# Half B of the first MoE layer and the whole second layer move from fp32r pairs to fp16 pairs, with gate tiles of 512 columns and layer 2 taken over quarters of d_ff

## The chip, the cores and the metric

One core of one Trainium2 chip (trn2). The metric is the device time of one execution in microseconds (us); lower is better. Five engines run side by side: TensorE (PE in the rows, with its weight loads as PEld), VectorE (DVE), ScalarE (ACT), GpSimd (POOL) and SyncE (SP), which here only issues DMAs.

## The reference, cut to what matters

```python
def _attn_ref(q, k, v, tau):                      # (4, 8, 576, 64), float32
    scores = 1.0 / np.sqrt(64) * np.matmul(q, k.transpose(0, 1, 3, 2))
    scores = np.where(scores >= scores.max(-1, keepdims=True) - tau, scores, -1e9)
    attn = softmax(scores)                        # with + 1e-09 under the division
    return np.matmul(attn, v)

def reference(...):
    x = attention, as (2304, 512)                 # tokens x d_model
    h = x @ moe_w_in                              # (512, 2048)
    x = (h * np.clip(h + 3, 0, 6) / 6) @ moe_w_out  # (2048, 512)
    h = x @ moe2_w_in
    return (h - np.tanh(h)) @ moe2_w_out
```

The four weight matrices come as float64; the kernel reads them as pairs of 32-bit words and makes float32 of them on ACT and DVE (`load_w`: one ACT and four DVE instructions of 512 columns for each 128 rows of d_ff).

## The kernel before, in words

Every product is made three times to keep float32 accuracy: each operand is a pair, a high and a low part, and high x high, high x low and low x high are added up in PSUM (`mm3`, L408). Before, both parts are fp32r tiles (float32 read in one pass).

The kernel has three stages, and a planner (`Plan`) writes out the order of every engine's instructions ahead of time: each task has an assumed duration, a key (a wanted start) and its buffers, and the planner plays them through and issues them in the order that comes out. On the chip the engines then run these queues strictly in order.

1. Attention, 144 units of 128 queries by 576 keys, with **half A** of layer 1 (the first 1024 of d_ff) woven in: PE makes scores (tile `s`), DVE takes the row maximum (L602), ACT the exponential (L604), DVE the cut (L613), POOL and ACT split the result into two fp16 parts, a DMA transposes them (`pt<-pp`), PE multiplies by v, itself an fp16 pair (`tp<-vt,pt`, L648). Half A's result goes to DRAM as `ys`, and its input as `xs`.
2. **Half B** of layer 1 (the other 1024 of d_ff): 9 blocks of 256 tokens x 8 tiles `m` of d_ff. `hidden` makes 12 matmuls of 256 columns into a PSUM tile (`m` or `h` by turns), `gate1` makes g on ACT and DVE (Relu L711, product L713, high part L718, low part L721), and `second` makes 12 matmuls of 256 columns into `ya`. Weights and x arrive as fp32r tiles; the blocks 0 and 1 take the first weights by turns, since the weights are still being made.
3. **Layer 2**, as Winograd's form of Strassen's product on blocks of 2 x 2: seven products of 6 matmuls of 256 columns, added up by DVE (`plus`, L1128) after an ACT copy (`keep`, L1123), then `gate2` (tanh L1135, difference L1136, L718, L721) and the output product with 3 matmuls of 512 columns for each tile of 128 tokens (`ya<-wo,g`). The stretches run over (half of d_ff, pair of token blocks p, quarter j of the half); the ninth block has a short stretch without Strassen. The parts of x are made in the first half, stored to DRAM (`xd..`) and read again in the second by POOL DMAs (L1111). The first half's partial output goes to DRAM (`po`, L1164) and is read and added in the second (L1169).

PSUM has two banks `m`, two `h` and four `ya`. The rings `R_t2` and `R_g2` hold the gates' tiles.

Of the kernel before, what the change touches and what calls it, by code (L numbers as in the profile page):

```python
# [43 lines left out]

class Ring:
# [16 lines left out]
class Plan:  # L62
# [13 lines left out]
    def add(self, eng, dur, key, fn, r=(), w=(), after=(), xfer=0.0, hold=False, slack=0.0, port=None):  # L76
        deps = dict.fromkeys(after)
# [111 lines left out]
def attention_moe_moe_kernel(  # L189
# [29 lines left out]
    nc = tc.nc  # L219
# [15 lines left out]
    HUGE = 122879.9921875  # L235

# [31 lines left out]
    three = const.tile([128, 1], F32, name="three")  # L268
# [12 lines left out]
    ident = at_p.tile([128, 128], F32, name="ident")  # L281
    ones = at_p.tile([128, 128], F32, name="ones")
# [56 lines left out]
    def load_w(kind, m, src, key, step, to, after=(), slack=0.0, scratch=None, cs=0.0, first=None, low="pool"):  # L339
# [12 lines left out]
        split_ = isinstance(to, list)  # L352

        def load():
# [5 lines left out]
            else:  # L360
# [4 lines left out]
            out=part(F32), in_=raw(1).bitcast(F32), func=ACTF.Abs), r=[wst], w=[wu], slack=cs if first is None else first)  # L365
# [10 lines left out]
                out=raw(1).bitcast(U32) if split_ else part(U32), in0=raw(0).bitcast(U32), scalar=29, in1=part(U32),  # L376
                op0=ALU.logical_shift_right, op1=ALU.bitwise_or),
        ]
        for n, f in enumerate(steps):
            add("dve", 0.65 if n > 1 or scratch else 0.5, key + 3 + n * step, f,  # L380
                r=[wu] if n < 2 else [wu, wst], w=[wst] if n == 3 and split_ else [wu], slack=cs, port=not scratch)
        if not split_:
            return add("dma", 0.47, key + 3 + 4 * step, lambda: nc.sync.dma_start(out=to, in_=part(F32)), r=[wu], xfer=0.8)
        n = DM // len(to)
        for h, W in enumerate(to):
            f32 = lambda h=h: raw(1)[:, h * n:(h + 1) * n].bitcast(F32)
            hi_lo(f32, W, [wst], key + 3 + 4 * step, step, n, cs, low)
# [10 lines left out]

    def flat(ap):
# [941 lines left out]
```

## Time and profile before

| | |
|---|---|
| time, three runs | 1111.94, 1113.19, 1115.34 us; median 1113.19 |
| the profiled execution | span 1113.7 us; no time of its own is listed beside the span |
| PE busy | 1047.2 us (94%), clock 0.975 of full on the mean |
| DVE, ACT, POOL busy | 825.4 (74%), 661.2 (59%), 352.3 (32%) us |
| DMA | 193.96 MB, mean 174 GB/s |
| chain that ended last | PE 80%, DVE 7%, DMA 5%, ACT 5% of the span |

PE's busy time is made of modelled ends of pipelined matmuls, so the mean duration of a matmul in the rows (395 ns for 512 columns) is longer than what one adds to the time; the start-to-start distance in a run of equal matmuls is what counts, and the chain of work that ended last gives it as a duration divided by a count.

### The profile page before, as it was taken

How to read it: one execution, taken by the hardware profiler on the slowest of the kernel's cores; microseconds unless marked ns; L12 is line 12 of the kernel's file. 1: busy time of each engine (PE TensorE's matmuls, PEld its weight loads, DVE VectorE, ACT ScalarE, POOL GpSimd, SP SyncE). 2: the span in 40 equal slices, each digit the busy share in tenths (PEclk: the TensorE clock that was granted, in tenths of full speed). 3: DMA queues.
4: the chain of work that ended last, by engine and by line, in shares of the span. 5: the costliest groups of instructions: out<-in, count | busy, mean ns of one | idle time of the engine just before them, and what ended most of it. 6: DMA issues, size and time to landing. Idle time of an engine off the chain costs nothing.

```text
span 1113.7 us, 23705 instructions
## 1 busy us (share of the span) xinstructions
PE 1047.2 (94%) x8912; PEld 975.8 (88%) x8912; DVE 825.4 (74%) x1761; ACT 661.2 (59%) x1420; POOL 352.3 (32%) x389
## 2 busy tenths in 40 slices
PE   5668799999999999989999999999999999999998
PEld 4557788998999899979999999988989898898887
DVE  5889977688878886757877776896796886656653
ACT  6867878688868886654544444654554564333332
POOL 2666757575766675662111100000000010010000
PEclk9858899999999999999999999999999999999999
DMA  7898678868987797778697765654732652543613
GB/s 182 164 224 203 132 180 168 188 130 189 171 173 134 176 146 152 168 214 250 208 292 242 231 195 169 236 180 141 266 130 86 227 202 77 187 136 83 193 47 95
DMA packets 283666, 193.96 MB, mean 174 GB/s; under 512 B 203424, under 2 KB 254112, under 8 KB 283552
## 3 DMA queue, kind: packets, MB, share of 16 engines
q1 hardware_dynamic: 268672, 166.50, 57.7%
q0 software_dynamic: 14256, 25.69, 8.1%
q8 instruction: 70, 1.15, 0.4%
q10 hardware_dynamic: 624, 0.26, 0.1%
q14 instruction: 44, 0.36, 0.1%
HBM read 96.99 MB, written 52.95 MB: 135 GB/s over the span
## 4 chain that ended last, share of the span: by engine, by line
PE 80%; DVE 7%; DMA 5%; ACT 5%; issue 2%; POOL 0%; SPq 0%; ACTq 0%; DVEq 0%; POOLq 0%
PE ya L408 26%; PE m L408 21%; PE h L408 10%; PE m L754 7%; PE s L597 7%; PE tp L648 6%; DVE e L613 2%; PE tp L480 2%; DMA pt<-pp 2%; DVE z L602 1%; DMA wdo<-wu 1%; DMA st<-in_moe_w_out_dram 1%; DMA st<-in_moe_w_in_dram 1%; ACT e L604 1%; ACT pp L618 1%
## 5 line engine op out<-in xcount | busy, mean ns | idle before, releaser
L408 PE MATMUL ya<-wo,g 128*128 128x512 f32 x864 | 238.0, 395 | 0.3 <-ACT g L718 0.3
L622 POOL TENSOR_TENSOR pp<-e,pp 128x128 f16<-128x128 f32 (+3 forms) x160 | 185.0, 1177 | 121.5 <-ACT pp L618 59.0
L408 PEld LDWEIGHTS m<-x,wi 128*128 128x128 f32 x1392 | 187.3, 189 | 12.5 <-ACT t L1123 0.3
L408 PE MATMUL m<-x,wi 128*128 128x256 f32 x1392 | 194.6, 281 | 0.1
L408 PEld LDWEIGHTS ya<-wo,g 128*128 128x128 f32 x864 | 146.7, 188 | 19.7 <-DVE wu L1169 0.8
L602 DVE TENSOR_REDUCE z<-s 128x1 f32<-128x576 f32 x144 | 108.4, 754 | 54.2 <-PE s L597 53.2
L408 PEld LDWEIGHTS h<-x,wi 128*128 128x128 f32 x1008 | 135.8, 190 | 7.8
L408 PE MATMUL h<-x,wi 128*128 128x256 f32 x1008 | 141.7, 282 | 0.0
L718 ACT ACTIVATE g<-t 128x256 fp32r<-128x256 f32 x216 | 89.4, 415 | 69.7 <-DVE t L1136 47.5
L613 DVE SCALAR_TENSOR_TENSOR e<-s,z,e 128x576 f32<-128x576 f32 x144 | 116.2, 812 | 15.4 <-ACT e L604 10.0
L408 PE MATMUL m<-xT,ai 128*128 128x256 f32 (+1 forms) x768 | 120.9, 303 | 3.1 <-DVE t L713 1.9
L597 PE MATMUL s<-ks,q 128*128 128x288 f32 x512 | 105.6, 335 | 18.7 <-DVE e L613 18.1
L721 DVE TENSOR_TENSOR g<-t,g 128x256 fp32r<-128x256 f32 x216 | 91.0, 422 | 40.5 <-ACT g L718 36.7
L408 PE MATMUL ya<-g,wo 128*128 128x256 f32 x864 | 115.6, 283 | 3.9 <-ACT g L718 3.2
L604 ACT ACTIVATE e<-s,z 128x576 f32<-128x576 f32 x144 | 105.5, 739 | 22.9 <-DVE z L602 18.3
L1135 ACT ACTIVATE t<-t 128x256 f32<-128x256 f32 x128 | 53.4, 417 | 106.5 <-DVE t L1128 105.9
L408 PEld LDWEIGHTS ya<-g,wo 128*128 128x128 f32 x864 | 108.3, 190 | 5.1 <-ACT g L718 3.8
L408 PEld LDWEIGHTS m<-xT,ai 128*128 128x128 f32 x768 | 107.5, 192 | 5.2 <-DVE t L713 2.7
L597 PEld LDWEIGHTS s<-ks,q 128*128 128x128 f32 x512 | 81.8, 211 | 25.8 <-issue 13.0
L648 PE MATMUL tp<-vt,pt 128*128 128x65 f16 (+1 forms) x2240 | 88.0, 199 | 9.3 <-DMA pt<-pp 6.2
L648 PEld LDWEIGHTS <-pt 128*128 128x128 f16 (+1 forms) x2240 | 79.6, 104 | 17.9 <-DMA pt<-pp 8.5
L618 ACT ACTIVATE pp<-e 128x1152 f16<-128x1152 f32 (+1 forms) x80 | 85.1, 1063 | 8.5 <-DVE e L613 7.0
(124 smaller groups left out, 1543.8 us busy)
## 6 DMA issues: line engine op xcount, KB each, us to landing
st<-in_moe_w_in_dram SPq DMA_DIRECT2D x32, 512.0 KB, 4.7
st<-in_moe_w_out_dram SPq DMA_DIRECT2D x32, 512.0 KB, 4.5
x<-xs POOLq DMA_DIRECT2D x36, 256.0 KB, 6.6
y<-y SPq DMA_DIRECT2D x18, 512.0 KB, 4.0
xs<-xT SPq DMA_DIRECT2D x8, 640.0 KB, 4.9
y<-ys SPq DMA_DIRECT2D x9, 512.0 KB, 5.8
po<-wu SPq DMA_DIRECT2D x18, 256.0 KB, 2.0
wu<-po SPq DMA_DIRECT2D x18, 256.0 KB, 2.9
```

Source lines behind the costliest of these rows:

```text
L408: nc.tensor.matmul(ps, l[a], r[b], start=first and t == 0 and i == 0, stop=last and t == 2 and i == n - 1,)
L597: nc.tensor.matmul(ps.t[:, half, 0:SH], l, ks[:, half * SH:(half + 1) * SH], start=i == 0, stop=i == len(ops) - 1,)
L602: add("dve", 0.69, key, lambda: nc.vector.tensor_reduce(out=z.t[:, 0:1], in_=s(), axis=AX.XY, op=ALU.max, negate=True), r=[ps], w=[z])
L604: exp = add("act", 0.66, key, lambda: nc.scalar.activation(out=ex(), in_=s(), func=ACTF.Exp, bias=z.t[:, 0:1]), r=[ps, z], w=[e])
L613: add("dve", 0.74, key, lambda: nc.vector.scalar_tensor_tensor(out=ex(), in0=s(), scalar=z.t[:, 1:2], in1=ex(), op0=ALU.is_ge, op1=ALU.mul ...
L618: high = add("act", t_act(w * S, sbuf=True), key, lambda: nc.scalar.activation(out=pp.t[:, 0:w, 0:S], in_=e.t[:, 0:w, :], func=ACTF.Copy), ...
L622: add("pool", t_pool(w * (src.stop - src.start)), key, lambda src=src, dst=dst: nc.gpsimd.tensor_tensor(out=pp.t[:, 0:w, dst], in0=e.t[:, ...
L648: nc.tensor.matmul(pv.t[0:m, w_ * (D + 1):(w_ + 1) * (D + 1)], pt.t[:, n, blk, rows], vv, start=o == 0, stop=o == len(ops) - 1)
L718: hi = add("act", t_act(n, sbuf=True), key, lambda: nc.scalar.activation(out=gh(), in_=t(), func=ACTF.Copy), r=[bt], w=[bh])
L721: add(low, t_pool(n) if low == "pool" else t_dve(n), key, lambda: eng.tensor_tensor(out=gl(), in0=t(), in1=gh().bitcast(F32), op=ALU.subtr ...
L754: prev = [add("pe", t_mm(n, 1), kd, lambda p=p, l=l, r=r, m=m, s=s, ps=ps: nc.tensor.matmul(ps.t[:, 0:n], W["o", m].t[:, l, s], r[m].t[:, ...
L1135: add("act", t_act(n), key, lambda: nc.scalar.activation(out=s_(), in_=h.t[:, 0:n], func=ACTF.Tanh), r=[h], w=[u])
```

## The change

Half B and layer 2 use fp16 tiles for both parts. An fp16 has a small range, so every operand is divided by a power of two found from the data (the row sums of its magnitudes, or for half B's weights the row maxima), and the gates undo it. The parts of the change:

- **The scales cross the partitions by PE.** ACT sums the magnitudes of a row (`row_sums`; for the weights of half B, 16 new loads `look` during attention with a DVE maximum each). `highest` turns the 128 sums into one row by a PE transpose, DVE takes the maximum, `everywhere` multiplies the one number by a row of ones on PE so that it stands on all partitions, and DVE makes the power of two. There are 24 such crossings: 9 for x in half B, 5 for x in layer 2, 10 for weights. They use the banks `m`.
- **fp16 matmuls**: 1728 of 256 columns in half B, 1536 of 256 and 864 of 512 in layer 2, as many as before. In the program each is now a weight load and a matmul; an fp32r matmul is one instruction that loads its own weights.
- **Gates of 512 columns**: one PSUM bank holds two tiles of d_ff, so half as many ACT and DVE instructions, each twice as wide; the ones with a scale per partition read it as an operand.
- **Layer 2 in four quarters** of d_ff, each with two tiles j at once; a stretch (quarter, p) has 84 matmuls of 256 columns and 48 of 512. The parts of x stay on chip for all four, so the stores and reads of `xd` go. Partial outputs are stored once (quarter 0), then added into DRAM by 36 accumulating DMAs from POOL (quarters 1 and 2), and read back in quarter 3. Their tiles `o` have three buffers.
- 18 of layer 2's 32 weight loads run in half B (28 before), the others in layer 2 up to the third quarter.
- x of half B is read by SP (before: POOL), then scaled and split (one ACT sum, one ACT copy and two DVE instructions of 1024 columns for each of 9 blocks).

The order on PE in the middle of layer 2, before: matmuls of `x` and `wi` into `m` and `h` (a Strassen product, 6 each) and output matmuls into `ya`.

```order
L408 MATMUL ya<-wo,g 128x512 x3
L408 MATMUL m<-x_14020,wi 128x256 x6
L408 MATMUL ya<-wo,g 128x512 x3
L408 MATMUL h<-x_14038,wi 128x256 x6
L408 MATMUL ya<-wo,g 128x512 x6
```

The same place now, at the seam between a Strassen product and the outputs; a product has 12 pairs and the outputs behind it 6.

```order
L472 LDWEIGHTS wi
L472 MATMUL m<-x_11486,wi 128x256
L472 LDWEIGHTS g
L472 MATMUL ya<-wo,g 128x512
...
L472 LDWEIGHTS wi
L472 MATMUL h<-x_11486,wi 128x256
```

Each matmul now has a weight load of its own in PE's queue; products and outputs alternate as before, in runs twice as long.

The order on PE around a crossing in half B, now (`xmax` holds the row sums of a block of x, `one` the maximum, `bw` and `bo` the weights); before, nothing stood between such runs of matmuls.

```order
L472 LDWEIGHTS bo
L472 MATMUL ya<-g,bo 128x256
L452 MATMUL m<-ident,xmax 1x128
L472 LDWEIGHTS bw
L472 MATMUL m<-xh,bw 128x256
...
L459 MATMUL m<-one,ones 128x1
L472 LDWEIGHTS bo
```

The transpose and the spread stand 12 pairs apart in this place; PE's queue stops at L452 if ACT's sum is late and at L459 if DVE's maximum is.

The order on POOL in layer 2: before, it read the parts of x again; now it adds the partial outputs `po` of 128 x 512 into DRAM.

```order
-L1111 DMA x_13485<-xd0T_184 128x1024
-L1111 DMA x_13505<-xd0X_185 128x1024
-L1111 DMA x_13525<-xd0T_186 128x1024
...
+L1413 DMA po_105<-o 128x512
+L1413 DMA po_106<-o 128x512
+L1413 DMA po_103<-o 128x512
```

31 reads went, 36 accumulating stores came; each frees a buffer `o` that an ACT copy waits for.

The diff, cut to its core:

```diff
+    def row_sums(src, dst, junk, r, w, key, n, cs=0.0):
+
+        return add("act", t_act(n, sbuf=True) + 0.19, key, lambda: nc.scalar.activation(
+            out=junk(), in_=src(), func=ACTF.Abs, scale=TOP, accum_out=dst), r=r, w=w, slack=cs)
...
+    def highest(src, top, key, after, ring):
+
+        bank = ring.new()
+        x = add("pe", 0.3, key, lambda: nc.tensor.transpose(bank.t[0:1, 0:128], src, ident), w=[bank], after=after)
+        return add("dve", 0.26, key + 0.1, lambda: nc.vector.tensor_reduce(
+            out=top, in_=bank.t[0:1, 0:128], axis=AX.X, op=ALU.max), r=[bank], w=[bank], after=[x])
+
+    def everywhere(top, key, after, ring, dur, fn):
+
+        bank = ring.new()
+        x = add("pe", 0.1, key + 0.2, lambda: nc.tensor.matmul(
+            bank.t[:, 0:1], ones[0:1, :], top, start=True, stop=True), w=[bank], after=after)
+        return add("dve", dur, key + 0.3, lambda: fn(bank.t[:, 0:1]), r=[bank], w=[bank], after=[x])
...
-    def mm3(ps, pairs, first=True, last=True, passes=(0, 1, 2)):
+    def mm3(ps, pairs, first=True, last=True, passes=(0, 1, 2), third=0, swap=0):
...
-            a, b = ((0, 0), (0, 1), (1, 0))[t]
+            a, b = ((0, 0), (swap, 1), (1, third))[t]
...
+        if far:
+            go = lambda: nc.vector.scalar_tensor_tensor(
+                out=gl(), in0=gh(), scalar=1.0 / GS2, in1=t(), op0=ALU.mult, op1=ALU.subtract)
+        else:
...
+            add("dma", 0.47, key, load, w=[wst], after=after, xfer=1.75, slack=ST)
+            seen[kind].append(add("dve", 0.69, key + 8.0, lambda: nc.vector.tensor_reduce(
+                out=mx[:, 5 + m:6 + m], in_=wst.t.rearrange("p (n t) -> p n t", t=2)[:, :, 1].bitcast(F32), axis=AX.X,
+                op=ALU.max, apply_absolute_value=True), r=[wst], slack=SB))
...
-        R_wi = ring2("slot1", 2 * MH, [128, 2, KD // 2, 128], F32R, "wi", 20)
-        R_wo = ring2("slot1", MH, [128, 2, DM], F32R, "wo", 2)
-        R_x2 = ring2("x2", 4, [128, 2, KD // 2, NB], F32R, "x2", 4)
-        R_t2 = ring2("g2", 2, [128, NB], F32, "t", 5)
-        R_g2 = ring2("g2", 3, [128, 2, NB], F32R, "g", 5)
-        R_f = ring2("big", 0, [128, 2, DM], F32, "f", 1)
-        R_c = ring2("big", 0, [128, DM], F32, "c", 4)
-        R_y = ring2("big", 0, [128, KD, NB], F32, "y", 3)
...
+        R_t2 = ring2([128, 2 * NB], F32, "t", tg=5, big=2)
+        R_g2 = ring2([128, 2, 2 * NB], F16, "g", tg=6, slot2=4)
+        R_bw = ring2([128, 2, DM], F16, "bw", slot1=MH)
+        R_bo = ring2([128, 3, DM], F16, "bo", slot1=MH)
...
+        R_wi = ring2([128, 2, 7, 2 * 128], F16, "wi", big=4)
+        R_wo = ring2([128, 3, DM], F16, "wo", big=8)
+        R_x = ring2([128, 2, 7, 2 * NB], F16, "x2", big=1, slot2=3)
...
+        R_o = ring2([128, DM], F32, "o", slot2=3)
...
+            a = row_sums(lambda: part(0), xmax[:, i:i + 1], lambda: x.t[:, 0, :, 0:n], [xf], [x], key - 10.0, KD * n)
+            a = common(xmax[:, i:i + 1], top_x[i % 2], xpow[:, 0, i:i + 1], xpow[:, 1, i:i + 1], 2.0 ** -6, key - 9.0, [a])
+            s = xpow[:, 1, i:i + 1]
+            hi = add("act", t_act(KD * n, sbuf=True, scalars=True), key - 6.0, lambda: nc.scalar.activation(
+                out=x.t[:, 0, :, 0:n], in_=part(0), func=ACTF.Copy, scale=s), r=[xf], w=[x], after=[a])
+            lo = add("dve", t_dve(KD * n, scalars=True), key - 5.0, lambda: nc.vector.scalar_tensor_tensor(
+                out=part(0), in0=part(0), scalar=s, in1=x.t[:, 0, :, 0:n],
+                op0=ALU.mult, op1=ALU.subtract), r=[x], w=[xf], after=[hi])
+            add("dve", t_dve(KD * n, scalars=True), key - 4.5, lambda: nc.vector.scalar_tensor_tensor(
+                out=x.t[:, 1, :, 0:n], in0=part(1), scalar=s, in1=part(0),
+                op0=ALU.mult, op1=ALU.add), r=[xf], w=[x], after=[lo])
+            u = lambda k: unscale[:, k, i:i + 1]
...
+            for a, m in enumerate(ms):
+                w = W["i", m]
+                pairs = lambda w=w: [
+                    ((w.t[:, 0, cols(kk)], w.t[:, 1, cols(kk)]), (x.t[:, 0, kk, 0:n], x.t[:, 1, kk, 0:n]))
+                    for kk in range(KD)]
+                turn[:] = [add("pe", t_half(n, 3 * KD), key + a * PM, lambda a=a, pairs=pairs: mm3(
+                    ps.t[:, a * n:(a + 1) * n], pairs(), first=a == 0, last=a == len(ms) - 1),
+                    r=[w, x], w=[ps], after=turn[-1:])]
+                hid.append(turn[-1])
+            gate1(lambda: ps.t, lambda: t.t, lambda: g.t[:, 0], lambda: g.t[:, 1],
...
-        order2 = [(half, p, j) for half in range(2)
-                  for p in ([0, NP2, *range(1, NP2)] if half == 0 else [*range(NP2), NP2]) for j in range(MQ)]
...
+        order2 = [(q, p) for q in range(NQ) for p in (first_order if q == 0 else [*range(NP2), NP2])]
...
-                xd[p, name] = dram.tile([128, 2, KD // 2, NB], F32, name=f"xd{p}{name}")
-                x_kept[p][name] = add("dma", 0.6, key + i + 2.0, lambda x=x, name=name: nc.sync.dma_start(
-                    out=xd[p, name], in_=x.t.bitcast(F32)), r=[x], xfer=1.6, slack=CF)
...
-        def again(p, key, after_y, after):
-
-            out = {}
-            for i, (name, stored) in enumerate(x_kept[p].items()):
-                x = out[name] = R_x2.new()
-                add("pool", 1.0, key + i - 6.0, lambda x=x, name=name: nc.gpsimd.dma_start(
-                    out=x.t, in_=xd[p, name].bitcast(F32R)), w=[x], after=[stored, *after], xfer=1.6, port=False)
-            return out
-
...
+            pair(lambda: ys_[0].t, four, [ys_[0]], [x], key - 2.0, 4 * n, s, ready, CL, CL, 0.2)
+            for i, name in enumerate(rows):
+                if name in ("X11", "X21"):
+                    continue
+                make(name, key + 2 * i - 3.0)
+                k = at_piece[name]
+                put = lambda h, k=k: x.t[:, h, k].rearrange("p (k n) -> p k n", k=2)
+                pair(src[name][0], put, [src[name][1]], [x], key + 2 * i - 2.0, 2 * n, s, ready, CL, CL, 0.2)
...
+            add("dve", t_dve(2 * NB, scalars=True), key, lambda: nc.vector.scalar_tensor_tensor(
+                out=s_(), in0=s_(), scalar=inv, in1=h.t, op0=ALU.mult, op1=ALU.subtract), r=[h, u], w=[u])
...
+            if q < NQ - 1:
+                add("act", t_act(DM, scalars=True), key, lambda: nc.scalar.activation(
+                    out=o.t, in_=a.t[:, 0:DM], func=ACTF.Copy, scale=sc), r=[a], w=[o], after=[ready])
+                if q == 0:
+                    po_stores[tile_] = add("dma", 0.47, key, lambda: nc.sync.dma_start(
+                        out=po[tile_], in_=o.t), r=[o], xfer=0.8)
+                else:
+                    po_stores[tile_] = add("pool", 1.0, key, lambda: nc.gpsimd.dma_start(
+                        out=po[tile_], in_=o.t, accum_op=ALU.add), r=[o], after=[po_stores[tile_]], xfer=1.6, port=False)
                 return
...
+            tiles = [(t, 0) for t in range(nb * nt)]
+            tiles += [(t, 1) for t in [*range(half, nb * nt), *range(half)]]
+            for t, a in tiles:
+                for j in range(MQ):
```

## Rows read from the trace of the kernel before

**Rows 1.** Busy time by stage: stretch, length, engines, clock, DMA share, GB/s.

```profile
core 0: us, PE busy (x) PEld busy (x) DVE busy (x) ACT busy (x) POOL busy (x), PEclk, DMA share, GB/s
290.00:450.00 160.00, 154.60 (x1763) 147.04 (x1762) 121.48 (x240) 119.64 (x224) 102.31 (x105) 1.00 0.81 155
512.00:600.00 88.00, 84.12 (x684) 82.92 (x683) 68.57 (x154) 41.44 (x91) 14.39 (x20) 0.98 0.86 262
600.00:690.00 90.00, 90.00 (x761) 90.00 (x760) 64.83 (x149) 40.01 (x92) 5.74 (x8) 1.00 0.64 202
722.00:930.00 208.00, 207.59 (x1317) 186.96 (x1317) 163.58 (x407) 113.05 (x283) 4.28 (x8) 1.00 0.49 174
930.00:1106.00 176.00, 175.99 (x1095) 157.41 (x1094) 103.65 (x249) 62.31 (x160) 12.17 (x23) 1.00 0.39 117
```

**Rows 2.** The chain that ended last: start us, us, what.

```profile
516.89 11.79 DMA st<-in_moe_w_out_dram
...
760.59 0.71 PE m L408 x6
...
763.43 2.79 PE ya L408 x12
...
1104.36 4.21 PE ya L408 x18
1108.57 0.02 issue
1108.59 0.69 DVE wu L1169
```

**Rows 3.** What PE waited for, 290 to 450, then 512 to 1114: us, times, longest.

```profile
PE s L597 <- DVE e L613: 1.6, 2, 0.8
PE tp L648 <- DMA pt<-pp: 1.6, 2, 1.3
...
PE ya L408 <- ACT g L718: 3.5, 3, 2.2
PE ya L408 <- DVE g L721: 0.4, 1, 0.4
```

**Rows 4.** Timeline of PE, 115 to 121: start us, us, what, count.

```profile
115.29 2.03 PE L648 MATMUL tp<-vt,pt 128*128 128x65 f16 x56
117.25 0.79 PE L597 MATMUL s<-ks,q 128*128 128x288 f32 x4
117.88 0.60 PE L480 MATMUL tp<-ident,qr 128*128 128x128 f32 x4
118.24 1.68 PE L408 MATMUL m<-xT,ai 128*128 128x256 f32 x12
...
120.28 0.28 PE L547 MATMUL tp<-vs,ones 128*128 128x1 f32 x2
120.42 0.84 PE L408 MATMUL m<-xT,ai 128*128 128x256 f32 x5
```

**Rows 5.** Groups by form: count | busy us, mean ns | idle before.

```profile
L547 PE MATMUL tp<-vs,ones 128*128 128x1 f32 x32 | 5.7, 248 | 2.6 <-ACT vt L545 1.5 <-DVE z L610 0.7 <-DVE m L367 0.4
L512 DVE SCALAR_TENSOR_TENSOR q<-tp,tau_b,q 128x512 fp32r<-128x512 f32 x32 | 23.8, 745 | 1.3 <-ACT q L510 1.3
L1095 DVE TENSOR_TENSOR c<-y 128x512 f32<-128x512 f32 x9 | 6.2, 685 | 0.0
L367 DVE TENSOR_SCALAR wu<-wu 128x512 f32<-128x512 f32 x48 | 24.0, 501 | 17.1 <-ACT wu L364 14.8
```

**Rows 6.** Timeline of DVE in layer 2: start us, us, what.

```profile
900.08 0.42 DVE L396 TENSOR_TENSOR wi<-c,wi 128x256 fp32r<-128x256 f32 x1
900.42 0.42 DVE L1136 TENSOR_TENSOR t<-t 128x256 f32<-128x256 f32 x1
900.75 0.42 DVE L396 TENSOR_TENSOR wi<-c,wi 128x256 fp32r<-128x256 f32 x1
```

**Rows 7.** What DVE waited for, 290 to 450.

```profile
DVE z L602 <- PE s L597: 22.7, 23, 3.9
```

**Rows 8.** DMA issues: count, KB each, median us from issue to landing.

```profile
st<-in_moe_w_in_dram SPq DMA_DIRECT2D x32, 512.0 KB, 4.7
x<-xs POOLq DMA_DIRECT2D x36, 256.0 KB, 6.6
po<-wu SPq DMA_DIRECT2D x18, 256.0 KB, 2.0
x<-xd0T POOLq DMA_DIRECT2D x4, 512.0 KB, 6.5
```

More of the change, by code (lines that the diff above doesn't have):

```diff
@@ L267, in attention_moe_moe_kernel @@
     tau_b = const.tile([128, 4], F32, name="tau_b")
-    three = const.tile([128, 1], F32, name="three")
+    NBL = len(blocks)
+    wm_t = const.tile([128, 2 * (5 + MH) + 8 * (5 + MH // 2)], F32, name="wmax")
+    widths = [(x, 5 + MH) for x in ("bi", "bo")] + [(k + str(q), 5 + MH // 2) for k in "io" for q in range(4)]
+    wmax = {x: wm_t[:, sum(w for _, w in widths[:i]):sum(w for _, w in widths[:i + 1])] for i, (x, _) in enumerate(widths)}
+    xmax = const.tile([128, NBL], F32, name="xmax")
+    xpow = const.tile([128, 2, NBL], F32, name="xpow")
+    unscale = const.tile([128, 2, NBL], F32, name="unscale")
+    ymax = const.tile([128, NBL], F32, name="ymax")
+    ypow = const.tile([128, 2, NBL], F32, name="ypow")
+    hid_s = const.tile([128, 2, 2, NBL], F32, name="hid_s")
+    out_s = const.tile([128, 2, NBL], F32, name="out_s")
+    one = const.tile([128, 4], F32, name="one")
+    three = const.tile([128, 2], F32, name="three")
+    ident = const.tile([128, 128], F32, name="ident")
+    ones = const.tile([128, 128], F32, name="ones")
     ps_m = ctx.enter_context(tc.tile_pool(name="ps_m", bufs=1, space=PSUM))
@@ L905, in load_x, with common @@
+        top_x = [one[0:1, a:a + 1] for a in range(2)]
+        def common(src, top, p, inv, c, key, after):
+            x = highest(src, top, key, after, R_m)
+            return everywhere(top, key, [x], R_m, 0.45, lambda b: power(b, p, inv, c))
+        def load_x(i, c, n, key):
+            xf, x = R_xf.new(), R_xh.new()
             after = writers(c, n)
+            part = lambda i: xf.t[:, i, :, 0:n]
             for h in range(2):
-                x = R_x2.new()
-                xs_.append(x)
@@ L947, in attention_moe_moe_kernel @@
+        for o, (kind, src) in enumerate((("i", w1_in), ("o", w1_out))):
+            for m in range(MH):
+                W = WB[kind, m] = (R_bw if kind == "i" else R_bo).new()
+                load_w(kind, MH + m, src, start - FW + WBO + WBS * (MH * o + m), 0.8, [W], late, cs=CB, first=CB1,
+                       put=scaled_pair(wmax["b" + kind][:, 2:3], scaled["b" + kind], kind == "o"))
         key = T2
         steps, xb, accs, before = [], {}, {}, {}
-        work = [(x, m) for m in range(MH // 2) for x in (0, 1)]
@@ L1217, in go @@
+                            third=2),
+                            r=[W, g], w=[ps], after=prevs.get((q, p, t), ()))
+                        prevs[q, p, t] = [x]
                         if l:
-                            finish(half, (2 * p * NB) // 128 + t, ps, key + 1.0)
+                            finish(q, (2 * p * NB) // 128 + t, ps, key + 1.0)
                     outs.append(go)
             return outs
+        nf = [NF]
+        for x in range(2):
+            record_prepare(x, [L2 - PK[2 * x], L2 - PK[2 * x + 1]], [[hid[-int(PK[2 * x] / 2.6) - 8]], [hid[-int(PK[2 * x + 1] / 2.6) - 8]]])
```

580 lines of the change are left out of this document (353 added, 227 removed).

## The prediction

> **What bounds the kernel now.** I read the busy time by stage first, because the change leaves attention nearly alone and rebuilds the rest. Attention ends near 512 us. From there PE is busy for all but 4 us of the first 88, and then for practically every microsecond to the end, at a granted clock of 1.00, the full of its two levels (2.4 GHz), while VectorE is busy 72 to 79% of the time and falls to 59% at the end, and the DMA engines 64%, then 39% [rows 1]. So behind 512 us a microsecond counts if it is PE's. The chain that ended last says the same: links of PE only, six matmuls of 256 columns in 0.71 us (118.3 ns each), twelve of 512 in 2.79 and eighteen in 4.21 us (233 ns each) [rows 2]; the stage from 600 us counts 761 in 90.00 us, 118.3 again [rows 1]. The sum is closed with these: 1728 + 1536 matmuls of 256 columns take 386.1 us and 864 of 512 take 201.3, together 587.4, and from 511.9 to the last matmul's end at 1108.6 us there are 596.7. Some 9 us are lost: PE waited 3.9 us for the gates [rows 3], mostly at 528 us, where a load of half B's weights took 11.79 us to land [rows 2], and the rest is spread.
>
> **fp16 matmuls.** The count of matmuls and columns stays, so what matters is what one adds. Between 256 and 512 columns an fp32r matmul costs (233 - 118.3) / 256 = 0.448 ns per column and 3.6 ns besides. The clock of 2.4 GHz would give 0.417 ns per column. The fixed 3.6 ns is small although each matmul loads new weights: that load lies beside the stream. I take it that the fp32r operand, not the array, makes the 0.031 ns per column more, and that fp16 streams at the clock with the same 3.6: 110.3 and 216.9 ns. That saves 3264 x 8.0 = 26.1 us and 864 x 16.1 = 13.9 us, **40.0 us**. No row shows an fp16 matmul of this width. The nearest is attention's, 65 columns wide: 56 from 115.29 to 117.25 us, 35.0 ns each [rows 4], and 65 columns at the clock are 27.1. If 7.9 ns is what a pair of weight load and matmul adds at any width, the new costs are 114.6 and 221.2 ns and the saving 22.3 us. Without any fixed cost (106.7 and 213.3) it is 54.9 us. If the column costs fp16 as much as fp32r, it is nothing. I take 40 because at 65 columns the stream is too short to hide a load, and at 256 it is four times as long; the ends are 0 and 54.9.
>
> Here the Trainium skill speaks on both sides. "TensorE: Matmul & The Clock Gate", section "Back-to-back issue gap", gives N/2.4 + 2.5 ns for a warm matmul; by that the saving would be an estimated 44.6 us. The same section says that a sustained stream of pairs of weight load and matmul takes about 81 ns at 128 columns, 25 more than that formula; 25 ns on each matmul here would be an estimated 131.7 and 238.3 ns, a loss of 48 us. The 35.0 ns of the fp16 pairs here, which leave 7.9 over the stream, speak against so much.
>
> **The crossings.** PE gets 24 transposes to one row and 24 spreads. In attention four transposes take (118.24 - 117.88) / 4 = 0.09 us each, and a spread by ones, which stands as two records, 0.14 us [rows 4]. That is 24 x 0.23 = **5.5 us**, on the path since PE has no gaps. Each also makes PE, which runs its queue in order, wait for ACT's sum and then for VectorE's maximum; behind it stand all products and outputs. Attention has the same construction 16 times, and PE idled 2.6 us ahead of it, 0.16 each [rows 5]. The planner puts 3 to 84 matmuls between the two halves in most places, none in four. From 0 to 2 x 24 x 0.16 = 7.7 us; I take one wait for each crossing, **3.9 us**.
>
> **The looks.** 16 loads of 512 KB and 16 maxima of 512 columns come into attention's last third. The maximum has no row; a VectorE instruction of 512 columns is 0.685 us [rows 5], together 11 us. VectorE waits 22.7 us for PE's scores between 290 and 450 us [rows 7], which covers them. The DMA engines are 81% busy there [rows 1], and a load of this size lands in 4.7 us [rows 8]; the transposes `pt` queue behind them. PE now waits only 1.6 us for those and 1.6 us for VectorE [rows 3]. From 0 to 11 us; I take **2 us**, near the bottom because both queues have room. If it is gone, scores come late first.
>
> **The start of half B.** Before, each tile m needed both its weights at once, and one late load stopped PE [rows 2]. Now all eight input weights come first, and the first output weight is needed only 84 pairs (9.3 us) after the start. I give back half of the 3.9 us waited, **2 us**; the ends are 3.9 back and 4 lost, if the eight output weights, which VectorE must now make in one run, are late.
>
> **The gates, x and weights on ACT and VectorE** I cost at nothing, with PE as cover. VectorE's work falls a little in sum (half as many gate instructions: 0.685 us for 512 columns, 0.745 with a scale per partition [rows 5], against 2 x 0.42 [rows 6]), but is uneven. Counting its rows in the new order at these durations, the full stretches of the first quarter, which also split x, take 18.6, 21.0 and 16.8 us, and two of the second quarter, in which the third is prepared, 20.8 and 23.8. PE needs 84 x 0.1103 + 48 x 0.2169 = 19.7 us for a stretch. Independent VectorE instructions start 0.33 us apart though each lasts 0.42 [rows 6]; 0.085 less for some 32 instructions leaves 16 to 21 us. It just fits; half B counts 189 us so, 160 without the overlap, against 190.6 of PE. The removal of the `xd` traffic (62 transfers of 512 KB) frees no PE time: the DMA engines were at 39 to 49% [rows 1].
>
> **The sum**, against the profiled execution: 1113.7 - 40.0 + 5.5 + 3.9 + 2 - 2 = 1083.1 us. Its span is 0.5 us over the median of the three runs, so **1083 us** stands for a run (1082.6, rounded). By its own terms the forecast runs from 1060 (54.9 saved, no crossing waits) to 1102 (all waits at their upper ends).
>
> **Rivals.**
> 1. *VectorE takes PE's place as the bound* in the first two quarters and at the end of half B. For it: the counts above, and a queue in order, where four chained instructions of a weight (the first 0.50 us, [rows 5]) stand ahead of a gate. If durations do not overlap, four stretches exceed PE's 19.7 us by 1.3, 1.1, 4.1 and 0.2, 7 us together, and with 5% of half B (9 us) PE loses 16: 1099 us. Against it: at 72 to 79% VectorE stopped nothing before. 15%.
> 2. *The weight load shows*: 22.3 us saved instead of 40, 1101 us. 8%.
> 3. *An fp16 column costs what an fp32r column does*: nothing saved, 1123 us, slower. The rows leave it open, since no wide fp16 matmul was run; the trace gives no other reason for 0.448 ns at full clock. 6%, with the 131.7 ns of the skill's sentence in it.
> 4. *The accumulating DMAs hold up the gates* (slower). In quarters 1 and 2 a stretch finishes four tiles `o`, with three buffers. Between the first and the fourth finish lie 18 output matmuls and two products, 3.9 + 2.6 = 6.5 us; the fourth ACT copy waits for the first tile's DMA, and behind it on ACT stand copies and gates. PE needs that bank 3.9 us later. So a DMA that lands within 10.4 us costs nothing, and each microsecond over it costs one in eight stretches; 30.6 us are eaten at 14.2 us. POOL's plain transfers of 256 KB landed in 6.6 us, SP's in 2.0, POOL's of 512 KB in 6.5 [rows 8]; an accumulating one has no row. At 16 us the time would be 1128. 6%. The Trainium skill, "SBUF — State Buffer", section "SBUF: two separate sides", says that GpSimd cannot write the descriptors of its DMAs while VectorE runs an instruction that takes both ports, a reason for such a delay; no row here separates it.
> 5. *The looks crowd attention's transposes* and take most of the gain: near 1110. 5%.
>
> **How the numbers follow.** The forecast has 60%. A change of under 0.3% (3.3 us) is about what runs of this kernel cannot tell from none. Faster: 60 + 15 + 8 and half of rival 5, 85%. Same: the rest of rival 5 and what lies between the cases, 5%. Slower: rivals 3 and 4 with their slighter forms, 10%. For the range I go down to 1062, just over the forecast's own floor, and up to 1104, which takes in rivals 1 and 2 at their prices; outside are rivals 3 to 5 and the upper half of rival 1's spread, 2 in 10.
>
> **What would show it.** In the new chain, twelve matmuls of 256 columns should be 1.32 us and three of 512 0.65; 1.42 and 0.70 would prove rival 3, 1.37 rival 2. PE's waits behind 512 us should name L452 and L459 with some 4 us, and the gates with a few; VectorE names in tens of microseconds would be rival 1, an ACT copy into `o` that waited for a DMA rival 4, with the landing time of `po<-o` beside it. Attention should end 0 to 4 us later than 512. I am wrong if PE idles over 15 us behind attention, or if the column of fp16 is not at the clock.

## The result, and the profile after

The changed kernel takes **1097.88 us** (median of four runs, 1096.08 to 1098.64) against 1112.57 us before (1111.20 to 1115.34), a ratio of 0.9857 with a 95% interval of 0.9832 to 0.9882. Its profiled execution took 1096.08 us, with a span of 1094.3 us.

The chain that ended last, in the kernel after (start us, us, what), answers to [rows 2]:

```profile
1071.10 5.18 PE ya L472 x24
1076.28 2.62 PE m L472 x24
1078.90 10.37 PE ya L472 x48
1089.27 0.03 issue
1089.30 0.75 DVE o L1418
```

Twenty-four matmuls of 256 columns take 2.62 us, 109.2 ns each, and 48 of 512 take 10.37 us, 216.0 ns each, where before it was 118.3 and 233. The end is still PE's.

Busy time by stage, kernel after (columns as in [rows 1]; the first five lines are its attention and the last half-A group, the others lie behind the start of half B):

```profile
330.00:360.00 30.00, 29.46 (x343) 28.12 (x340) 23.27 (x47) 23.45 (x47) 19.40 (x21) 1.00 0.86 189
360.00:390.00 30.00, 25.22 (x261) 22.34 (x260) 26.53 (x52) 22.53 (x41) 17.47 (x17) 0.83 0.91 196
390.00:450.00 60.00, 58.44 (x632) 56.09 (x631) 47.91 (x93) 42.53 (x79) 36.21 (x38) 1.00 0.96 198
450.00:480.00 30.00, 28.41 (x332) 27.09 (x332) 19.95 (x47) 16.98 (x34) 15.76 (x16) 1.00 0.92 211
480.00:512.00 32.00, 23.50 (x182) 21.11 (x178) 18.52 (x41) 16.34 (x31) 10.05 (x10) 0.74 0.64 192
...
530.00:600.00 70.00, 69.26 (x627) 60.82 (x626) 60.88 (x118) 48.15 (x81) 0.00 (x0) 1.00 0.64 202
600.00:720.00 120.00, 119.41 (x1080) 105.46 (x1078) 99.49 (x207) 78.49 (x140) 0.00 (x0) 1.00 0.59 196
720.00:780.00 60.00, 56.83 (x417) 40.31 (x415) 55.39 (x121) 37.97 (x60) 0.00 (x0) 1.00 0.31 106
780.00:930.00 150.00, 150.00 (x1024) 99.96 (x1022) 115.42 (x219) 93.11 (x166) 15.72 (x18) 1.00 0.53 134
930.00:1089.00 159.00, 159.00 (x1054) 102.86 (x1052) 101.67 (x178) 71.53 (x118) 15.53 (x18) 1.00 0.47 102
```

Behind half B's start PE is as full as before, at clock 1.00; only at the start of layer 2 (720 to 780 us, VectorE 55.39 of 60 us busy) does it lose 3.2 us. Ahead of it two stretches are new: from 360 to 390 us the granted clock is 0.83, and from 480 to 512 PE is busy 23.50 of 32 us at 0.74. In the kernel before, the same two stretches were:

```profile
360.00:390.00 30.00, 27.52 (x310) 25.40 (x309) 25.96 (x55) 24.79 (x47) 19.12 (x19) 1.00 0.77 178
480.00:512.00 32.00, 30.45 (x193) 29.84 (x194) 21.93 (x42) 17.43 (x37) 13.70 (x16) 0.95 0.81 232
```

When half B starts is told by PE's timeline of the kernel after: the last products of attention and the first matmuls of half B.

```profile
486.02 1.76 PE L712 MATMUL tp<-vt,pt 128*64 128x65 f16 x28 [2.92 <-DMA pt<-pp]
...
530.20 2.79 PE L472 MATMUL m<-xh,bw 128*128 128x256 f16 x24
```

The same two in the kernel before:

```profile
475.88 1.08 PE L648 MATMUL tp<-vt,pt 128*64 128x65 f16 x28 [1.50 <-DMA pt<-pp]
...
511.93 1.59 PE L408 MATMUL m<-x,wi 128*128 128x256 f32 x12
```

So attention ends 10 us later and half B starts 18.3 us later: what fp16 gives, the first half of the kernel partly takes back. From its start half B and layer 2 now take 559.05 us (530.20 to 1089.25), against 596.7 before.

What PE waited for from 530 us on, kernel after (us, times, longest), answers to the second part of [rows 3]:

```profile
PE ya L472 <- DVE g L792: 1.8, 3, 0.7
PE m L459 <- DVE one L453: 1.5, 2, 0.9
PE m L452 <- ACT xh L439: 0.6, 1, 0.6
PE ya L472 <- ACT g L788: 0.4, 1, 0.4
```

The crossings (L452, L459) cost 2.1 us in waits, the gates 2.2. The accumulating transfers that rival 4 rests on, from the DMA issues of the kernel after between 800 and 1094 us (count, KB each, median us from issue to landing):

```profile
po<-o POOLq DMA_DIRECT2D x36, 256.0 KB, 4.2
```

They land in 4.2 us, and none took longer than 8.4, under the 10.4 that were free. Last, how a crossing looks among fp16 matmuls, PE's timeline of the kernel after:

```profile
713.35 0.27 PE L452 MATMUL m<-ident,ymax 128*1 128x128 f32 x1
713.46 2.78 PE L472 MATMUL m<-xh,bw 128*128 128x256 f16 x24
716.17 0.38 PE L459 MATMUL m<-one,ones 1*128 1x1 f32 x2
716.48 2.79 PE L472 MATMUL ya<-g,bo 128*128 128x256 f16 x24
719.11 2.78 PE L472 MATMUL h<-xh,bw 128*128 128x256 f16 x24
```

From one start to the next the transpose takes 0.11 us. The 24 matmuls behind it take 24 x 0.1092 = 2.62 us, so they end at 716.08; the spread starts 0.09 later and its successor 0.31 after that. A crossing costs 0.11 + 0.09 + 0.31 = 0.51 us on PE, not 0.23.

### The profile page after: what moved, and what is told of

It is laid out like the page before. It is cut to its first block, busy times and chain, and to the rows that moved or that the text cites. A ratio compares the mean times of both kernels' runs of the same rounds, so it can differ in the third digit from the quotient of the medians.

```text
span 1094.3 us, 23286 instructions
## 1 busy us (share of the span) xinstructions
PE 1018.4 (93%) x8984; PEld 840.6 (77%) x8984; DVE 848.7 (78%) x1625; ACT 719.3 (66%) x1312; POOL 341.8 (31%) x358
## 4 chain that ended last, share of the span: by engine, by line
PE 57%; DVE 3%; ACT 2%; DMA 2%; issue 0%; POOL 0%; SPq 0%; ACTq 0%; DVEq 0%
PE ya L472 24%; PE m L472 16%; PE h L472 9%; PE m L828 3%; PE s L661 2%; PE tp L712 2%; DMA pt<-pp 1%; DMA f<-wdi 1%; PE m L459 1%; DVE t L1369 0%; PE tp L754 0%; ACT t L779 0%; DVE x L1273 0%; DVE t L782 0%; DVE g L792 0%
## 5 line engine op out<-in xcount | busy, mean ns | idle before, releaser
L472 PE MATMUL ya<-wo,g 128*128 128x512 f16 x864 | 205.4, 379 | 1.0 <-DVE g L792 0.6
L472 PEld LDWEIGHTS <-wi 128*128 128x128 f16 x1536 | 149.9, 98 | 40.4
L472 PEld LDWEIGHTS <-g 128*128 128x128 f16 x864 | 84.1, 98 | 79.3 <-DVE g L792 1.1
L472 PE MATMUL ya<-g,bo 128*128 128x256 f16 x864 | 101.4, 273 | 1.4 <-DVE g L792 1.2
L472 PE MATMUL m<-x,wi 128*128 128x256 f16 x768 | 95.3, 273 | 0.0
L472 PEld LDWEIGHTS <-bo 128*128 128x128 f16 x864 | 83.9, 98 | 11.8 <-issue 1.6
L1378 ACT ACTIVATE t<-t,hid_s 128x512 f32<-128x512 f32 x72 | 51.6, 718 | 62.3 <-DVE t L1369 61.7
L472 PEld LDWEIGHTS <-bw 128*128 128x128 f16 x864 | 84.1, 98 | 10.2 <-DVE t L782 0.2
L788 ACT ACTIVATE g<-t 128x512 f16<-128x512 f32 x108 | 67.0, 624 | 32.2 <-DVE t L1380 25.9
L792 DVE SCALAR_TENSOR_TENSOR g<-g,t 128x512 f16<-128x512 f16 x108 | 73.8, 686 | 17.6 <-ACT g L788 16.9
```

The source lines that it names most:

```text
L472: nc.tensor.matmul(ps, l[a], r[b], start=first and t == 0 and i == 0, stop=last and t == 2 and i == n - 1,)
L788: hi = add("act", t_act(n, sbuf=True), key, lambda: nc.scalar.activation(out=gh(), in_=t(), func=ACTF.Copy, scale=GS2 if far else 1.0), r= ...
L792: go = lambda: nc.vector.scalar_tensor_tensor(out=gl(), in0=gh(), scalar=1.0 / GS2, in1=t(), op0=ALU.mult, op1=ALU.subtract)
L1378: add("act", t_act(2 * NB, sbuf=True, scalars=True), key, lambda: nc.scalar.activation(out=s_(), in_=h.t, func=ACTF.Tanh, scale=c), r=[h], ...
```

## Experiments

Times are medians of four runs (e12: five, e10: eight, e11: six), each measured against runs of the kernel before taken with it, whose medians were 1112.6 to 1113.2 us. The last two columns are read from PE's timeline of one profiled execution of each: where attention's last products and half B's first matmuls start.

| kernel | time us | ratio, 95% interval | last products | half B |
|---|---|---|---|---|
| before | 1112.6 | 1 | 475.88 | 511.93 |
| after | 1097.9 | 0.9857 (0.9832-0.9882) | 486.02 | 530.20 |
| e1 no looks | 1080.5 | 0.9710 (0.9689-0.9731) | 474.48 | 515.65 |
| e2 looks earlier | 1096.1 | 0.9850 (0.9819-0.9881) | 486.92 | 529.26 |
| e4 stores later | 1097.4 | 0.9858 (0.9839-0.9876) | 487.58 | 530.93 |
| e5 split later | 1099.8 | 0.9877 (0.9861-0.9894) | 487.19 | 528.90 |
| e6 loads only | 1098.7 | 0.9872 (0.9857-0.9886) | 489.68 | 533.37 |
| e7 maxima only | 1083.4 | 0.9730 (0.9712-0.9748) | 474.62 | 516.97 |
| e9 small loads | 1095.9 | 0.9858 (0.9840-0.9876) | 487.19 | 530.70 |
| e12 looks unplanned | 1089.5 | 0.9793 (0.9772-0.9814) | 480.27 | 522.51 |
| e10 looks by POOL | 1117.3 | 1.0030 (1.0005-1.0055) | 508.17 | 552.62 |
| e11 looks by ACT | 1106.8 | 0.9948 (0.9929-0.9967) | 500.40 | 543.71 |
| e3 no crossings | 1083.4 | 0.9740 (0.9725-0.9754) | 489.90 | 531.57 |
| e8 neither | 1068.1 | 0.9600 (0.9586-0.9614) | 474.50 | 514.71 |

**First round: where do the 18 us ahead of half B come from?** The chain of the kernel after suggested two places.

```profile
471.04 8.51 DMA pt<-pp
...
482.80 3.18 DMA pt<-pp
...
505.17 1.16 ACT xh L1040
506.35 1.28 DVE xf L1042
...
508.00 1.27 DVE xh L1045
...
510.77 1.20 DVE xh L1045
511.97 0.41 DVE t L782
...
512.42 3.44 PE m L472 x12
```

One transpose `pt` lands after 8.51 us; three 512-KB weight loads were issued just ahead of it on SP's queue, and ahead of those a store of layer 1's output held the queue. And the splits of x stand on VectorE ahead of the gate product `t` that PE waits for. At 512 us twelve matmuls of 320 columns take 3.44 us, 287 ns each; at 387.66 us, in the same kernel, twelve of the same width took 1.84. From 480 to 512 us PE had idled 8.5 us, and the granted clock had fallen to a mean of 0.74.

In the diffs "..." marks what is left out, and the remarks behind # are mine. e1, half B's weight scales as constants, no looks:

```diff
-    LOOK, LOOKS = 92, 3
+    LOOK, LOOKS = 9999, 3
...
-            scaled["b" + kind] = everywhere(mx[0:1, 4:5], k0 + 0.3, [top], R_m, 0.3, scales)
+            scaled["b" + kind] = add("dve", 0.2, k0, fixed)   # memset of the scale and its inverse
```

> The 16 looks and the two crossings of half B's weight scales are gone; the two scales are fixed powers of two, equal to those that would be found. In the kernel after, attention's last transposes on PE end at 487.8 us and half B starts at 530.4, against 477.0 and 511.9 before. Theory Q (SP's queue: a store of layer 1's output ahead of the transposes holds the queue from 461 to 466 us, three weight loads behind it fall on the last transposes of pt, which land after 8.5 us; the looks changed that order): the last transposes end at 477 to 480, half B starts at 519 to 523, and the time is 1087 to 1091. Theory T (the looks' 8 MB of traffic as such): the same. Theory X (the split of x stands ahead of the last gates of half A and costs the other 7.6 us): half B does not start before 518. If the looks are innocent: 487 and 530, and 1096 to 1098.

e2:

```diff
-    LOOK, LOOKS = 92, 3
+    LOOK, LOOKS = 60, 3
```

> All 16 looks stay, but begin at attention's unit 60 instead of 92, some 85 us earlier; SP's order around the last transposes then has no store of layer 1's output ahead of them. Theory Q: as without the looks, last transposes at 477 to 480 us, half B at 519 to 523, 1087 to 1091. Theory T (traffic as such, 8 MB wherever it stands): attention still ends 8 us or more late, 485 to 488, 1095 to 1098, PE's waits for pt only moved to an earlier stretch.

e4, the stores of layer 1's output in half A:

```diff
-            y_stores[b, g].append(add("dma", 0.47, kd, lambda y=y, part=part: nc.sync.dma_start(
+            y_stores[b, g].append(add("dma", 0.47, kd + 6.0, lambda y=y, part=part: nc.sync.dma_start(
```

> The looks stay where they are; layer 1's output stores get a key 6 us later, so that SP issues the last transposes of pt ahead of them instead of behind. Theory Q: last transposes end at 478 to 482 us, half B at 520 to 525, 1088 to 1093. Theory T: no change, 487, 530, and 1096 to 1098.

e5:

```diff
-    XL3 = 40.0
+    XL3 = 24.0
```

> The loading and the split of half B's first two blocks of x get a key 16 us later, so that on VectorE the gate products of the last half-A tiles stand between the parts of the split, not behind them all. Theory X (the split ahead of the gates costs 7.6 us): attention's last transposes stay at 487 to 488 us, half B starts at 523 to 526, 1091 to 1094. Rival V (VectorE has too much work there in sum, the eight weight chains included, so a moved split only moves the wait): half B stays at 529 to 532, 1096 to 1099, with PE waiting for xh or bw instead of the gate product.

The looks, with the two crossings of their scales, cost 17.4 us (1097.9 to 1080.5), more than the 15 by which the forecast was low. But theory Q fell. What SP waited for in the kernel after between 452 and 490 us shows the store that held the queue:

```profile
SPq L838 <- ACT t L836: 6.0, 2, 5.0
```

In e2 and in e4 the stores make SP wait 0.4 us or less there, and nothing was gained (1096.1 and 1097.4). Nor did theory X give a gain: in e5 half B starts 1.3 us earlier and the whole is not faster. Rival V, that VectorE has too much to do there in sum, comes nearer with its time, but its sign did not show: PE still waits for the gate product `t` (2.2 us from 490 to 530 us, 2.7 in the kernel after) and not for `xh` or `bw`. Theory T seemed to hold: the looks cost the same when the first is issued at 214 us (e2) instead of 313. It didn't last.

**Second round: which part of a look?** In e6 the maxima are left out, in e7 the loads; in both, as in e1, the two scales are constants.

```diff
 e6
-            seen[kind].append(add("dve", 0.69, key + 8.0, lambda: nc.vector.tensor_reduce(
...
 e7
-            add("dma", 0.47, key, load, w=[wst], after=after, xfer=1.75, slack=ST)
...
+                out=mx[:, 5 + m:6 + m], in_=ident[:, 0:1].to_broadcast([128, DM]), axis=AX.X,
```

> The 16 loads of the looks stay at their places, the 16 maxima on VectorE are left out; half B's two weight scales are fixed numbers, as in the kernel without looks (1080.5 us). Theory T (the loads' traffic of 8 MB and SP's queue): 1094 to 1098, attention's last transposes end at 485 to 488 us. Theory V (the maxima, 16 x 0.677 = 10.8 us in VectorE's queue, which the softmax chain stands in): 1080 to 1083, last transposes at 475 to 478.

> The 16 maxima of 512 values stay in VectorE's queue, but read a constant, and the 16 loads are left out; half B's two weight scales are fixed numbers. Theory T: 1080 to 1083, last transposes at 475 to 478 us. Theory V: 1091 to 1097, last transposes at 484 to 488. If each is half of it: both kernels near 1088.

The loads alone cost as much as the whole looks (1098.7), the maxima little: 1083.4 against 1080.5, with overlapping intervals. The prediction's reading of [rows 7], that VectorE's waits cover eleven microseconds of maxima, was right but for these 2.9 us, which are not clear of noise.

**Third round: what about a load?** e9 issues loads of 8 KB at the same places (maxima left out, scales constant); what the planner reckons for them stays, so each engine's order is that of e6 but for the loads themselves.

```diff
...
-                    nc.sync.dma_start(out=wst.t, in_=src[f0:f0 + 128, :])
+                nc.sync.dma_start(out=wst.t[:, 0:16], in_=w1_out[f0:f0 + 128, 0:16])
```

> As the kernel with the looks' loads only (1098.7 us), with the 16 loads at the same places in SP's queue, but each of 8 KB instead of 512 KB (128 rows of 64 bytes); the maxima are left out, half B's two weight scales are fixed numbers. Theory B (the bytes: 8 MB more for DMA engines that are 69 to 92% busy): 1080 to 1084, DMA share from 330 to 480 us back to 0.70 to 0.88, last transposes at 475 to 478. Theory I (the issues: 16 more entries in SP's queue and the order that the planner makes around them): 1094 to 1098, last transposes at 485 to 489.

e10 and e11 let another engine issue the full loads:

```diff
-            add("dma", 0.47, key, load, w=[wst], after=after, xfer=1.75, slack=ST)   # nc.sync
+            add("pool", 1.0, key, load, w=[wst], after=after, xfer=1.75, slack=ST, port=False)   # e10, nc.gpsimd
+            add("act", 0.6, key, load, w=[wst], after=after, xfer=1.75, slack=ST, port=False)   # e11, nc.scalar
```

> The kernel after with all its computation, but POOL issues the looks' loads instead of SP. Theory B: the bytes stay, so 1094 to 1099, last transposes at 484 to 488. Theory L (a transpose waits in line behind a load that was issued ahead of it on SP's queue): 1081 to 1088, last transposes at 475 to 479. If POOL's issues hold up its subtractions for pp, above 1099.

> The kernel after with all its computation, but ACT issues the looks' loads. Theory B: 1094 to 1099. Theory L: 1082 to 1090; ACT's queue then holds the exponentials behind an issue that waits for its staging buffer, which would show as PE's waits for e and take back up to 10 us.

Theory T, in its form B, is gone as the main cause: with a sixty-fourth of the bytes the time is 1095.9, 2.8 us under e6 with all of them, and the intervals overlap. The windows of e9 (columns as in [rows 1]) show it beside those of e1.

e9:

```profile
360.00:390.00 30.00, 25.37 (x271) 22.51 (x270) 24.70 (x50) 22.70 (x41) 16.33 (x17) 0.89 0.69 130
...
480.00:512.00 32.00, 24.08 (x186) 21.31 (x186) 15.14 (x34) 16.26 (x30) 9.36 (x10) 0.74 0.66 196
```

e1:

```profile
360.00:390.00 30.00, 27.52 (x310) 25.42 (x309) 25.96 (x54) 24.79 (x46) 18.96 (x19) 1.00 0.78 180
390.00:450.00 60.00, 59.79 (x688) 57.54 (x687) 43.31 (x88) 43.58 (x82) 38.96 (x40) 1.00 0.84 146
...
480.00:512.00 32.00, 27.68 (x166) 25.94 (x166) 21.81 (x41) 17.16 (x32) 7.32 (x8) 0.89 0.82 256
```

From 360 to 390 us the DMA engines of e9 have less to do than those of e1 (0.69 against 0.78), and still PE has a hole there: it idles nearly twice as long (4.6 us against 2.5), and the clock falls to 0.89. Theory L gave no gain either: away from SP the loads made it worse, 1117.3 and 1106.8. These two runs do not refute it, though, since the planner wrote another order for each of them too. In e10 ACT waited 17.4 us for `pt`, up to 7.3 at once; why so long was not pursued.

**Fourth round: the order.** What e6 and e9 share is the planner's reckoning. It moves all transfers through one modelled pipe, and a transpose holds SP's queue to the end of it:

```
end = moving = max(moving, now + 1.3) + t.xfer
if t.hold:
    free[e] = max(free[e], end - 0.9)
```

Sixteen looks of 1.75 us put 28 us into that pipe in a stretch of some 135, and the planner writes another order around them. Ahead of half B, PE's written order has some 7010 matmuls and weight loads. Of these, 541 of the kernel after and 573 of e6 and e9 stand outside the longest sequence that they have in common with e1 (two instructions count as the same where the operation, the tiles without their buffer numbers and the addresses agree); of e7 it is 246. In e12 the looks are whole, loads and maxima, but aren't tasks of the planner: each is emitted behind an instruction that is there anyway. Beside the new instructions themselves, none is moved on any engine.

```diff
-            add("dma", 0.47, key, load, w=[wst], after=after, xfer=1.75, slack=ST)
-            seen[kind].append(add("dve", 0.69, key + 8.0, lambda: nc.vector.tensor_reduce(
...
+            behind(after[0], load)              # the transpose of unit u - 6
...
+                    behind(t, most)             # the last VectorE task of unit u + 4
+                    seen[kind].append(t)
```

> All of the looks is there, 16 loads of 512 KB and 16 maxima, and the whole computation of the kernel after; but the planner doesn't know of them: each load is issued right behind a transpose of pt, each maximum right behind a VectorE instruction of a later unit, so that every engine's order is that of the kernel without looks, with these rows put in. Theory O (what costs the time is the order that the planner writes when it reserves transfer time for the looks; neither bytes nor maxima nor entries in the queue): 1081 to 1086, last transposes of attention end at 475 to 479 us. Theory I (the entries in SP's queue themselves, which wait for a staging buffer or for their descriptors): 1092 to 1098, last transposes at 484 to 488. Bytes and maxima without order or entries would be above 1086 and below 1092.

It is neither theory O nor theory I: 1089.5 us falls between them, in the band that was left for bytes and maxima, and its interval meets neither that of after nor that of e1. Its windows:

```profile
360.00:390.00 30.00, 27.71 (x309) 25.22 (x308) 26.70 (x55) 24.94 (x46) 19.00 (x19) 1.00 0.95 230
390.00:450.00 60.00, 56.54 (x653) 53.87 (x652) 44.65 (x92) 40.86 (x76) 37.40 (x38) 1.00 1.00 200
...
480.00:512.00 32.00, 26.44 (x169) 24.48 (x170) 21.88 (x43) 18.03 (x33) 9.09 (x10) 0.84 0.70 222
```

With the DMA engines 95% busy, more than in after, PE keeps 27.71 us and the full clock between 360 and 390; e9, with a sixty-fourth of the bytes, has the hole. So the hole there came from the order, not from the traffic.

The two causes do not add up. Without the planner's order the looks still cost 9.0 us (e12 against e1); the planner's order with loads of hardly any bytes costs 15.4 (e9 against e1); both together cost 17.4, so that taking the order away from the whole looks gives back only 8.4 (after against e12). Compared by the ratios, 9.0 and 8.4 become 9.2 and 7.1, each uncertain by some 3.5 us, an estimate from the intervals.

Where the looks cost time in an unchanged order, PE's waits in e12 from 330 to 532 us show in part:

```profile
PE tp L712 <- DMA pt<-pp: 3.3, 3, 1.2
PE m L459 <- DVE wmax L1125: 2.3, 2, 1.9
```

The 3.3 us are waits for the transposes, all between 390 and 450 us, where the DMA engines are busy the whole time (share 1.00) and PE 56.54 us; in e1 the share is 0.84, PE is busy 59.79 us and does not wait for them there (its one wait for a transpose, 1.5 us, comes at 474 us). The 2.3 us are waits at the two crossings of the weight scales, which e1 lacks. Together, less e1's 1.5, this is 4.1 of the 5.8 us by which e12's last products come later than e1's. Single comparisons give about 2.9 us to the maxima (e7 against e1) and 2.8 to the bytes (e6 against e9), neither clear of noise.

e12 computes all that the kernel after does, and is the fastest here that does.

**The crossings** were priced apart.

```diff
...
-            x = highest(src, top, key, after, R_m)
-            return everywhere(top, key, [x], R_m, 0.45, lambda b: power(b, p, inv, c))
+            return add("dve", 0.3, key + 0.3, fixed, after=after)   # memset of 2 ** e and 2 ** -e
```

> The looks stay. The scales of x, y and of layer 2's weights are fixed powers of two, equal to those that would be found: 22 crossings less (transpose, maximum, spread, power on TensorE and VectorE); ACT's sums stay. By the trace after, a crossing takes PE 0.11 us for the transpose and 0.40 for the spread with the changes of operands around them, and PE waited 2.1 us for them behind 530 us: 22 x 0.51 + 2.1 = 13 us, so 1083 to 1087. By the prediction's 0.23 and 0.16 each it is 8.6 us, so 1088 to 1091.

> No looks and no crossings: all scales are fixed powers of two, equal to those that would be found. If looks and crossings add up: 1080.5 - 13 = 1067 (1065 to 1070) by the price of 0.51 each, 1072 (1070 to 1074) by the prediction's price. What is left over the 1713.7 terms then is the split of x and the weights in the last half-A group: half B still starts 2 to 4 us later than the 511.9 of before.

(The figure of 1713.7 in the last text is a slip; the terms of the sum are meant.) e3 gains 14.5 us, e8 12.3 on e1, and both times lie in the range for the price of 0.51. (e3's profiled execution was the longest of its four; between the two profiled executions the gain is 10.9.) From half B's first matmul to the end of the last, e3 takes 1078.66 - 531.57 = 547.1 us against 559.05: 12.0 us for the 20 crossings that lie there, 0.60 each, waits included. Looks and crossings add up within 2 us: e8 gains 29.8, e1 and e3 together 31.9.

## Why the prediction was right, and where it was off

The time fell, inside the range; the forecast of 1083 was some 15 us low. That it lies in the range is in part luck: the looks cost more than the 11 us that were their upper end, and the top of the range was drawn for rivals 1 and 2, which did not come. In the profiled execution, against its sum:

- **fp16 matmuls**: 40.0 us forecast; 3264 x 9.1 + 864 x 17.0 = 44.4 measured, 4.4 better. The argument held: fp16 streams at the clock, without fp32r's extra cost per column, and what a matmul adds besides is smaller still, 109.2 - 106.7 = 2.5 ns and 216.0 - 213.3 = 2.7. The formula in the Trainium skill, "TensorE: Matmul & The Clock Gate", section "Back-to-back issue gap", gives 2.5 and agrees with this trace. The figures of the Trainium skill in the same section for sustained pairs of weight load and matmul do not help here: about 81 ns at 128 columns, which no run here shows at that width, and about 131 ns at 512, which the prediction left aside and which is far under the 216.0 measured. (25 ns over the formula would also have been 134.2 and 240.8 ns, not the prediction's 131.7 and 238.3.) Rivals 2 and 3 fell.
- **Crossings**: 5.5 + 3.9 = 9.4 forecast for 24, 12.0 measured for the 20 behind half B's start. The wrong part is the price, taken from fp32 neighbours in attention [rows 4]: 0.23 against 0.51 on PE. The waits were less than allowed, 2.1 instead of 3.9.
- **Behind half B's start** PE lost 9.3 - 2 + 9.4 = 16.7 us by the forecast, and 559.05 - 543.0 = 16.0 in the trace. Gates, x and weights were hidden as said, but for 3.2 us at layer 2's start; rival 1 fell but for that, and rival 4 with the 4.2 us of `po`, at most 8.4.
- **The looks, 2 us**: this step failed. Half B starts at 530.2 instead of 511.9 + 2, 16.3 us late. The looks are 14.6 of the 18.3 us (530.20 to 515.65 in e1). It failed in two ways. It did not ask what the planner does with the new tasks, although the order was there to be read: the new order, with loads of hardly any bytes, costs 15.4 us (e9 against e1). And the price near the bottom, "because both queues have room", was too low in an unchanged order too, 9.0 us (e12 against e1): the DMA engines had no room from 390 to 450 us, where the transposes came late, and the two weight crossings made PE wait 2.3 us, not the 0.16 each of [rows 5]. For VectorE's maxima it was about right: 2.9 us, not clear of noise. Rival 5, that the looks crowd the transposes, is a part of this (3.3 us of waits in e12), but not most: with the small loads of e9 the DMA engines have room, and the time is that of after within 2 us.
- **The last half-A group**, costed at nothing under x and weights: without looks it still takes 515.65 - 474.48 = 41.2 us against 36.1 before. In e8, where its crossings are gone too, it is 40.2; the other 4 us I put to the split ahead of the gates, by the chain alone, since e5 did not get them back.

So 1083.1 - 4.4 - 0.7 + 16.3 = 1094.3, the span measured. These terms are 11.2 us; the rest of the 15 is not a term of the kernel but the choice of executions. In each run here whose own time is known, the time lies 1.7 to 1.9 us above its span. The profiled execution before has a span 1.1 us above the median time of its four runs, so it was one of the longer ones; after, the profiled one was the shortest of four, and its span lies 3.6 us under the median. The two spans differ by 19.4 us, the medians by 14.7.

What stays open: which of the moved instructions makes the hole at 360 us (the count alone does not tell: in e7 246 are moved, and it is 2.9 us over e1), where the rest of the 9 us of e12 goes, and why POOL and ACT do worse as issuers.

## What to carry over

Where a planner writes the order, a small task can cost more by what it does to the order than by what it lasts: compare the written orders ahead of a prediction, and try the new instructions once outside the planner's reckoning. And room in a queue is a matter of the stretch: a mean share of 0.81 did not show that the DMA engines would be full from 390 to 450 us once the looks were there. A price taken from other neighbours can be far off: a spread cost 0.14 us among fp32 matmuls and 0.40 among fp16 ones. And a gain behind a boundary is only kept if the work put ahead of it doesn't move the boundary: read when the stage starts before summing what it saves.

## What was unexpected of the hardware

A short run of PE idling cost more than itself, by the granted clock. Kernel after, stretches of 6 us (columns as before):

```profile
366.00:372.00 6.00, 4.31 (x50) 3.42 (x49) 4.71 (x8) 4.40 (x8) 3.41 (x5) 1.00 0.67 151
372.00:378.00 6.00, 4.11 (x62) 3.89 (x63) 5.81 (x12) 4.18 (x9) 4.88 (x4) 0.72 0.89 212
378.00:384.00 6.00, 5.13 (x45) 4.21 (x44) 5.70 (x14) 3.81 (x5) 2.95 (x4) 0.58 1.01 229
384.00:390.00 6.00, 5.67 (x61) 5.08 (x59) 4.81 (x8) 5.15 (x11) 5.66 (x5) 0.85 0.78 152
```

And e1, without looks:

```profile
366.00:372.00 6.00, 5.54 (x78) 5.07 (x75) 5.18 (x10) 4.38 (x9) 4.60 (x5) 1.00 0.50 128
372.00:378.00 6.00, 4.94 (x61) 4.55 (x60) 5.68 (x13) 5.11 (x11) 4.80 (x5) 1.00 0.72 161
378.00:384.00 6.00, 5.04 (x35) 4.23 (x35) 5.64 (x13) 5.94 (x12) 3.17 (x3) 1.00 0.86 164
```

PE idled 3.6 us of the first twelve in after, and the clock, which has two levels (1.2 and 2.4 GHz), went to a mean of 0.72 and then 0.58 before it recovered; in e1 PE idled 1.5 and the clock stayed at 1.00. At mean 0.83, the 25.22 busy us from 360 to 390 do the work of about 21, an estimate of 4 us lost to the clock beside the 4.8 idle. The waits listed for PE in that stretch come to 4.7 us: they are the idle time, and what the clock took stands in none of them.
